# Products of a unit as one run behind its turns, in a fused attention and two-layer feed-forward kernel on one core

## The chip, the core and the metric

The kernel runs on one core of one Trainium2 chip. The metric is the device time of one execution in microseconds (us). The core has five engines that work side by side, each through its own queue in order: PE (TensorE, matrix products; its weight loads are listed apart as PEld), DVE (VectorE), ACT (ScalarE), POOL (GpSimd) and SP (SyncE, which here only issues transfers; its queue is listed as SPq).

## The reference

Decay attention over 4 batches and 8 heads of 576 tokens with 64 features, then two feed-forward layers on the 2304 x 512 result:

```python
scores = scale * q @ k.T + (cum[i] - cum[j])      # cum: running sum of log f; causal mask
attn   = softmax(scores);  x = attn @ v           # heads side by side: 2304 x 512
h = x @ w_in;   g = h * tanh(softplus(h));   y = g @ w_out          # 512 -> 2048 -> 512
m = max(y @ w1, y @ w2, y @ w3);   out = m @ w2_out                 # 512 -> 768 -> 512
```

All of it is fp32, and the feed-forward inputs are split in a high and a low part so that one product is three (`mm3`, L179).

## The kernel before

**Attention.** `attention()` (L437) goes through 16 jobs, a job being one batch and one pair of heads (`U` and `L`: partitions 0 to 63 and 64 to 127), and each job has two units: g = 0 holds query rows 0 to 255, g = 1 the other 320. A unit is made in two halves. `scores` (L334) multiplies q and k into `sc`, DVE adds the decay and finds the row minimum (L386), ACT takes the exponent (L392) and POOL scales by the row sum (L356), which gives tiles `P`. Two units later (`LEAD`) `av` (L400) turns the `P` tiles with PE transposes into banks `pp` (L413, the "turns"; up to four per bank, 6 turns in a unit g = 0, 19 in a unit g = 1), copies each bank to `TA` or `TB` by DVE and ACT in turn (L417, L419), and multiplies with v into the accumulator `av` (L423, the "products"). A product uses 64 columns of the PE array, the lower 64 for head U and the upper 64 for head L; a unit g = 0 has 4 products, a unit g = 1 has 18 (6 of 256 columns, 2 of 128, 10 of 64). The trace lists an fp32 product as two rows (passes), so the 18 products are 36 rows. The finished accumulator is split by ACT and DVE into `xh` and `xl` (L131, L137), the input of the next layer. `prep` (L298) turns the next job's q and k (`tr`, L308 and L310) in each unit g = 0.

**What stands between.** `h_steps` (L475) makes the first layer's `h` (L181 to L183, full-array products) as soon as a block of 512 tokens is complete; two steps follow every unit. Weights come through `load_w_in` (L198): `fetch` issues a transfer on SP (L146), three ahead of use, and `convert` and `split` unpack them on ACT (L156), POOL (L160, L137) and DVE.

**What sets the order.** The code is written unit by unit, and a scheduler orders each engine's instructions by priority and its own estimate; attention has a high priority. `tc.issue_after(x)` (through `queued`, L176) keeps an instruction behind x on the engine. `att_psum` (L228) gives `pp` and `tr` three banks in common; the accumulator has one. After attention the rest runs stage by stage: `h` to its end, `y` (w_out), `g` (three maxima), `q` and `o`.

Of the kernel before, what the change touches and what calls it, by code (L numbers as in the profile page):

```python
# [34 lines left out]
LEAD = 2  # L35
# [25 lines left out]
LAYOUT = [turned_layout(g) for g in range(2)]  # L61
# [3 lines left out]
def tile_decay_attention__mish_ff__max3_ff(  # L65
# [16 lines left out]
    nc = tc.nc  # L82
# [10 lines left out]
    at = ExitStack()  # L93
# [8 lines left out]
    ident = const.tile([128, 128], F32, name="ident")  # L102
# [38 lines left out]
    def fetch(pool, src, bufs):  # L141

        m, n = src.shape[0] // 128, src.shape[1]
        r = pool.tile([128, m, n, 2], I32, name="wr", tag="wr", bufs=bufs)
        with queued(pace):
            nc.sync.dma_start(  # L146
                r.rearrange("p m n w -> p m (n w)"), src.bitcast(I32).rearrange("(m p) w -> p m w", p=128)
            )
        return r

    def convert(pool, r, bufs=None, abs_eng="dve"):

        t = pool.tile([128, r.shape[1], r.shape[2]], F32, name="wt", tag="wt", bufs=bufs)
        lo, hi, ti = r[:, :, :, 0], r[:, :, :, 1], t.bitcast(I32)
        if abs_eng == "act":
            nc.scalar.activation(t, hi.bitcast(F32), AF.Abs)  # L156
        else:
            nc.vector.tensor_scalar(ti, hi, 0x7FFFFFFF, None, op0=ALU.bitwise_and)
        eng = nc.gpsimd if abs_eng == "act" else nc.vector
        eng.tensor_scalar(  # L160
            t, t, F32_MIN_AS_HIGH_HALF, F32_MAX_AS_HIGH_HALF, op0=ALU.max, op1=ALU.min
        )
        nc.vector.tensor_scalar(
            ti, ti, 3, 0x3FFFFFF8, op0=ALU.logical_shift_left, op1=ALU.bitwise_and
        )
        nc.vector.scalar_tensor_tensor(
            out=ti, in0=hi, scalar=-0x40000000, in1=ti,
            op0=ALU.bitwise_and, op1=ALU.bitwise_or,
        )
        nc.vector.scalar_tensor_tensor(  # L170
            out=ti, in0=lo, scalar=29, in1=ti,
            op0=ALU.logical_shift_right, op1=ALU.bitwise_or,
        )
        return t

    def queued(last):  # L176
        return tc.issue_after(last[-1].ins) if last else ExitStack()
# [20 lines left out]
    def load_w_in():  # L198
        jobs = [(fp, c) for fp in range(NFP) for c in range(0, KD, 2)]
        raws = []  # L200
        for k, (fp, c) in enumerate(jobs):
            for f_, c_ in jobs[len(raws):k + 3]:
                raws.append(fetch(wst, moe_w_in[c_ * 128:(c_ + 2) * 128, f_ * 256:f_ * 256 + 256], 4))
            t = convert(wst, raws[k], abs_eng="act")
            split(wi[fp][:, 0, c:c + 2], wi[fp][:, 1, c:c + 2], t, "act", "pool")
            if c + 2 == KD:
                loaded.add(fp)
            yield
# [20 lines left out]
        return aps.tile([128, 512], F32, name=name, tag="ps", bufs=3)  # L229

    U, L = slice(0, 64), slice(64, 128)


    sums = [aw.tile([128, 5], F32, name=f"sums{i}") for i in range(4)]
    raws = [[ap_.tile([128, 640], F32, name=f"raw{c}{i}") for c in "qk"] for i in range(2)]
    vs = [aw.tile([128, 640], F32, name=f"vs{i}") for i in range(3)]
# [61 lines left out]
    def prep(J):  # L298

        b, hp, raw = J["b"], J["hp"], J["raw"]  # L300
        qq = as_.tile([128, 512], F32, name="qT", bufs=2)
        kk = as_.tile([128, S], F32, name="kT", bufs=2)
        last, v_ = q4[J["i"] % 2], vs[J["i"] % 3]
        rest = att_psum("tr")
        for i, dst in ((1, kk), (0, qq)):
            tr = att_psum("tr")
            for c in range(4):
                nc.tensor.transpose(tr[:, c * 128:c * 128 + 128], raw[i][:, c * 128:c * 128 + 128], ident)  # L308
            nc.scalar.activation(dst[:, 0:512], tr, AF.Copy)  # L309
            nc.tensor.transpose(rest[:, i * 64:i * 64 + 64], raw[i][U, 512:640], ident[U, U])  # L310
        nc.scalar.activation(kk[:, 512:S], rest[:, 64:128], AF.Copy)
        for h, rows in enumerate((U, L)):
            nc.scalar.activation(last[rows, h * 64:h * 64 + 64], rest[rows, 0:64], AF.Copy)
        for h in range(2):
            nc.sync.dma_start(
                v_[:, h * 256:(h + 1) * 256].rearrange("p (t d) -> p t d", t=4),
                v[b, 2 * hp + h, 0:512, :].rearrange("(t p) d -> p t d", t=4),
            )
        nc.sync.dma_start(
            v_[L, 512:640].rearrange("p (h d) -> p h d", h=2),  # L320
            v[b, 2 * hp:2 * hp + 2, 512:S, :].rearrange("h p d -> p h d"),
        )
        J.update(q=qq, q4=last, k=kk, vs=v_)
        mask_decay(J)
# [75 lines left out]
    def av(J, g, P):  # L400


        q0 = 0 if g == 0 else 256
        gw = 256 if g == 0 else 320
        T = (TA, TB)[g]
        acc = aps.tile([128, 512], F32, name="av", bufs=1)
        for c, blocks, products in LAYOUT[g]:
            pp = att_psum("pp")
            for n, (kt, h, qt) in enumerate(blocks):

                k0 = kt * 128 if kt < 4 else S - 128
                Pt = P[4] if qt == 4 else P[h, qt]
                nc.tensor.transpose(pp[:, n * 128:n * 128 + 128], Pt[:, k0:k0 + 128], ident)  # L413
            w = len(blocks) * 128
            count["bank"] += 1
            if count["bank"] % 2:
                nc.vector.tensor_copy(T[:, c:c + w], pp[:, :w])  # L417
            else:
                nc.scalar.activation(T[:, c:c + w], pp[:, :w], AF.Copy)  # L419
            for kt, off, w, *at in products:  # L420
                for h in range(2):
                    n = 4 * h + kt if kt < 4 else 8 + h
                    nc.tensor.matmul(  # L423
                        acc[(U, L)[h], off:off + w], J["vs"][:, n * 64:n * 64 + 64], T[:, at[h]:at[h] + w],
                        start=kt == 0 and off == 0, stop=kt == (1 if g == 0 else 4), skip_group_check=True,
                    )
        t0 = J["b"] * S + q0
        at_ = 0
        while at_ < gw:
            blk, off = divmod(t0 + at_, BLK2)  # L430
            n = min(gw - at_, BLK2 - off)
            xh, xl = x_tiles(blk)
            cs = slice(off, off + n)
            pace[:] = [split(xh[:, J["hp"], cs], xl[:, J["hp"], cs], acc[:, at_:at_ + n], "act", "dve")]
            at_ += n

    def attention():  # L437


        jobs = [(b, hp) for b in range(B) for hp in range(H // 2)]  # L440
        J = {0: load(0, *jobs[0])}
        yield 0
        prep(J[0])
        J[1] = load(1, *jobs[1])
        tok = 0
        units = [(ji, g) for ji in range(len(jobs)) for g in range(2)]
        pend = []
        for n in range(len(units) + LEAD):
            if n == 6 + LEAD:
                eps.clear()  # L450
                early.close()
                eps_h.append(sa.enter_context(tc.tile_pool(name="hps", bufs=2, space=PSUM, reuse_waits="tile")))
            if n < len(units):
                ji, g = units[n]
                pend.append((J[ji], g, scores(J[ji], g)))
            if n >= LEAD:
                unit = pend.pop(0)
                av(*unit)
                if unit[0]["hp"] == H // 2 - 1:
                    tok = unit[0]["b"] * S + (256, S)[unit[1]]  # L460
            if n < len(units):
                if g == (ji == 0) and ji + 1 < len(jobs):
                    prep(J[ji + 1])
                if g == 1 and ji + 2 < len(jobs):
                    J[ji + 2] = load(ji + 2, *jobs[ji + 2])
            yield tok
# [46 lines left out]
    credit, na = 0.0, 0  # L513
    while True:

        with tc.high_priority(AHEAD):
            done = next(attn, None)
        if done is None:
            break

        na += 1
        for _ in range(2 if 2 <= na <= 9 else 0):
            next(wgen, None)
        if len(loaded) == NFP and not x4:
            top.close()
            x4.append(top.enter_context(tc.tile_pool(name="x4", bufs=1)))
            x4[0].tile([128, 216], F32, name="gap")
        credit += RATE
        while credit >= 1.0:
            credit -= 1.0  # L530
            if next(steps, None) is None:
                credit = 0.0
# [113 lines left out]
    for step, (ib, fp, a) in enumerate(todo):  # L646
        n = blocks1[ib][1]
# [128 lines left out]
    for ft in range(NF2):  # L776
        g = [gps[ft % 2].tile([128, BLK2], F32, name=f"g{m}") for m in range(3)]
        for m in range(3):
            for c in range(KD):
                w = wa[m][ft // 3, c // 2]  # L780
# [26 lines left out]
    for t0 in (BLK2, BLK2 + 2 * HALF):  # L807
        hh = [hp2.tile([128, 2 * HALF], F32R, name=f"hh{c}") for c in range(NF2)]
        hl = [hp2.tile([128, 2 * HALF], F32R, name=f"hl{c}") for c in range(NF2)]
        for p in range(3):  # L810
# [54 lines left out]
            for i, eng in ((0, "pool"), (2, "dve"), (1, "dve"), (3, "dve")) if p == 2 else ((i, "pool") for i in range(4)):  # L865
                f, h = p + 3 * (i // 2), i % 2
# [37 lines left out]
```

## Time and profile before

| | |
|---|---|
| median of 3 runs | 925.68 us (924.67 to 927.26) |
| profiled execution, its own time | 926.2 us |
| span in its trace | 924.4 us (1.8 us lie around it) |
| instructions | 13929 |
| PE busy | 903.4 us, 98% of the span |
| DVE, ACT, POOL busy | 496.3, 400.1, 234.0 us |

A span is cut in windows below, and a timeline row gives the start, the duration and the number of merged rows. Matmuls overlap their neighbours in the trace, so the time that a row takes from the engine is read from start to next start, not from its duration.

### The profile page before, as it was taken

How to read it: one execution, taken by the hardware profiler on the slowest of the kernel's cores; microseconds unless marked ns; L12 is line 12 of the kernel's file. 1: busy time of each engine (PE TensorE's matmuls, PEld its weight loads, DVE VectorE, ACT ScalarE, POOL GpSimd, SP SyncE). 2: the span in 40 equal slices, each digit the busy share in tenths (PEclk: the TensorE clock that was granted, in tenths of full speed). 3: DMA queues.
4: the chain of work that ended last, by engine and by line, in shares of the span. 5: the costliest groups of instructions: out<-in, count | busy, mean ns of one | idle time of the engine just before them, and what ended most of it. 6: DMA issues, size and time to landing. Idle time of an engine off the chain costs nothing.

```text
span 924.4 us, 13929 instructions
## 1 busy us (share of the span) xinstructions
PE 903.4 (98%) x4800; PEld 711.8 (77%) x4800; DVE 496.3 (54%) x1186; ACT 400.1 (43%) x913; POOL 234.0 (25%) x317
## 2 busy tenths in 40 slices
PE   5898999999999999999999999999999999999998
PEld 3566666666666677889888888889888998889986
DVE  3688665334434442991267757584874455515440
ACT  4786656444444432442556545453443213312211
POOL 3689985222213220000002000000121323013310
PEclk9999999999999999999999999999999999999999
DMA  8896654333332113872365666663599543334401
GB/s 180 230 214 175 198 173 115 102 114 107 105 95 92 61 48 132 306 247 91 126 213 192 212 212 213 209 235 105 164 339 328 157 131 101 117 102 127 126 29 62
DMA packets 125030, 145.25 MB, mean 157 GB/s; under 512 B 64736, under 2 KB 78048, under 8 KB 124960
## 3 DMA queue, kind: packets, MB, share of 16 engines
q1 hardware_dynamic: 105856, 102.41, 37.8%
q10 hardware_dynamic: 16416, 27.79, 8.2%
q0 software_dynamic: 2688, 14.16, 4.2%
q8 instruction: 38, 0.62, 0.3%
q14 instruction: 32, 0.26, 0.1%
HBM read 102.83 MB, written 41.49 MB: 156 GB/s over the span
## 4 chain that ended last, share of the span: by engine, by line
PE 94%; DVE 2%; DMA 2%; issue 1%; ACT 1%; SPq 1%; DVEq 0%
PE h L181 8%; PE h L182 7%; PE h L183 7%; PE y L183 7%; PE y L181 7%; PE y L182 7%; PE av L423 7%; PE sc L332 6%; PE pp L413 6%; PE q L182 5%; PE q L183 5%; PE q L181 5%; PE o L181 3%; PE o L182 3%; PE o L183 2%; PE tr L308 2%
## 5 line engine op out<-in xcount | busy, mean ns | idle before, releaser
L182 PE MATMUL h<-xl,wi 128*128 128x512 f32 (+1 forms) x320 | 120.6, 377 | 1.8 <-DVE xl L137 1.8
L181 PE MATMUL h<-xh,wi 128*128 128x512 f32 (+1 forms) x320 | 122.0, 382 | 0.0
L183 PE MATMUL h<-xh,wi 128*128 128x512 f32 (+1 forms) x320 | 120.2, 376 | 0.0
L182 PE MATMUL y<-gl,wo 128*128 128x512 f32 (+1 forms) x320 | 117.7, 368 | 0.0
L183 PE MATMUL y<-gh,wo 128*128 128x512 f32 (+1 forms) x320 | 117.6, 368 | 0.0
L181 PE MATMUL y<-gh,wo 128*128 128x512 f32 (+1 forms) x320 | 106.3, 368 | 0.0
L638 DVE TENSOR_TENSOR gl<-g,gh 128x512 fp32r<-128x512 f32 x72 | 49.9, 695 | 91.7 <-ACT gh L637 91.3
L356 POOL TENSOR_SCALAR P<-P,rr 128x128 f32<-128x128 f32 (+3 forms) x128 | 74.8, 598 | 95.3 <-DVE rr L354 54.1
L392 ACT ACTIVATE P<-P,mn 128x128 f32<-128x128 f32 (+3 forms) x128 | 70.6, 554 | 62.6 <-DVE mn L386 62.6
L631 ACT ACTIVATE g<-g 128x512 f32<-128x512 f32 x72 | 45.4, 633 | 76.4 <-DMA g<-h_d 70.5
L182 PEld LDWEIGHTS h<-xl,wi 128*128 128x128 f32 x320 | 60.2, 188 | 12.9 <-issue 2.2
L181 PEld LDWEIGHTS h<-xh,wi 128*128 128x128 f32 x320 | 60.0, 188 | 12.7 <-issue 2.8
L183 PEld LDWEIGHTS h<-xh,wi 128*128 128x128 f32 x320 | 60.4, 189 | 10.5 <-issue 1.3
L182 PEld LDWEIGHTS y<-gl,wo 128*128 128x128 f32 x320 | 60.3, 188 | 10.2
L183 PEld LDWEIGHTS y<-gh,wo 128*128 128x128 f32 x320 | 60.3, 189 | 10.1
L181 PEld LDWEIGHTS y<-gh,wo 128*128 128x128 f32 x320 | 60.3, 189 | 10.1
L413 PE MATMUL pp<-ident,P 128*128 128x128 f32 x320 | 57.7, 290 | 3.6 <-ACT qT L309 3.6
L423 PE MATMUL av<-TB,vs 128*64 128x64 f32 (+2 forms) x576 | 60.4, 294 | 0.3 <-DVE xl L137 0.3
L413 PEld LDWEIGHTS pp<-ident,P 128*128 128x128 f32 x320 | 38.1, 143 | 24.6 <-issue 8.9
L830 DVE TENSOR_TENSOR u<-q,p 128x448 f32<-128x448 f32 x36 | 22.4, 622 | 63.2 <-PE q L183 63.2
L501 ACT ACTIVATE he<-h 128x512 f32<-128x512 f32 x56 | 33.1, 593 | 49.5 <-PE h L183 49.5
L423 PEld LDWEIGHTS av<-TB,vs 128*64 128x64 f32 x576 | 34.9, 136 | 25.3 <-issue 9.7
(141 smaller groups left out, 1880.6 us busy)
## 6 DMA issues: line engine op xcount, KB each, us to landing
g<-h_d SPq DMA_DIRECT2D x72, 256.0 KB, 2.9
s<-s_d SPq DMA_DIRECT2D x72, 256.0 KB, 2.9
h_d<-he ACTq DMA_DIRECT2D x56, 256.0 KB, 2.7
wr<-in_moe_w_out_dram SPq DMA_DIRECT2D x22, 512.0 KB, 4.4
wr<-in_moe_w_dram SPq DMA_DIRECT2D x24, 384.0 KB, 3.7
s_d<-sk POOLq DMA_DIRECT2D x12, 768.0 KB, 5.7
cb<-cum_d SPq DMA_DIRECT2D x32, 256.0 KB, 4.2
wr<-in_moe_w_in_dram SPq DMA_DIRECT2D x16, 512.0 KB, 4.4
```

What stands on the lines that cost most here:

```text
L181: nc.tensor.matmul(ps, wh, xh, start=start, stop=False, skip_group_check=True)
L182: nc.tensor.matmul(ps, wh, xl, start=False, stop=False, skip_group_check=True)
L183: return nc.tensor.matmul(ps, wl, xh, start=False, stop=stop, skip_group_check=True)
L332: nc.tensor.matmul(dst, lhs, J["k"][rows, c0:c0 + w], start=True, stop=True, skip_group_check=True)
L356: nc.gpsimd.tensor_scalar(made[ci], made[ci], rr[:, ci:ci + 1], 1.0, op0=ALU.mult, op1=ALU.mult)
L392: nc.scalar.activation(Pt, Pt, AF.Exp, scale=-1.0, bias=mn[:, col - 1:col], accum_out=sm[:, ci:ci + 1],)
L413: nc.tensor.transpose(pp[:, n * 128:n * 128 + 128], Pt[:, k0:k0 + 128], ident)
L423: nc.tensor.matmul(acc[(U, L)[h], off:off + w], J["vs"][:, n * 64:n * 64 + 64], T[:, at[h]:at[h] + w], start=kt == 0 and off == 0, stop=kt ...
L501: nc.scalar.activation(he, h, AF.Copy)
L631: nc.scalar.activation(g, g, AF.Mish)
L638: on_dve[:] = [nc.vector.tensor_tensor(out=gl, in0=g, in1=gh, op=ALU.subtract)]
L830: add = lambda eng, o, x, y: eng.tensor_tensor(out=o, in0=x, in1=y, op=ALU.add)
```

## The change

The change has two parts. In batches 1 to 3 a unit's products are no longer emitted bank by bank between its turns, but all together after its last turn, and, where the unit also holds a `prep`, after that `prep`'s last transposes (`last_tr`). The next unit's turns and `prep` transposes are issued behind the last of these products (`last_av`). In batch 0 (`together` is false) the products stay bank by bank. `prep`'s two 64-row transposes are now emitted ahead of the ACT copy and in the same queue hold. The second part lets `load_w_in` issue its first three transfers and then pause, in the first step of the main loop, where before nothing was done; the conversions keep their steps.

```diff
@@ load_w_in
             for f_, c_ in jobs[len(raws):k + 3]:
                 raws.append(fetch(wst, moe_w_in[c_ * 128:(c_ + 2) * 128, f_ * 256:f_ * 256 + 256], 4))
+            if k == 0:
+                yield
             t = convert(wst, raws[k], abs_eng="act")
@@ prep
-            for c in range(4):
-                nc.tensor.transpose(tr[:, c * 128:c * 128 + 128], raw[i][:, c * 128:c * 128 + 128], ident)
+            with queued(last_av):
+                for c in range(4):
+                    nc.tensor.transpose(tr[:, c * 128:c * 128 + 128], raw[i][:, c * 128:c * 128 + 128], ident)
+                last_tr[:] = [nc.tensor.transpose(rest[:, i * 64:i * 64 + 64], raw[i][U, 512:640], ident[U, U])]
             nc.scalar.activation(dst[:, 0:512], tr, AF.Copy)
-            nc.tensor.transpose(rest[:, i * 64:i * 64 + 64], raw[i][U, 512:640], ident[U, U])
@@ av
+        def multiply(products):
+            for kt, off, w, *at in products:
+                for h in range(2):
+                    n = 4 * h + kt if kt < 4 else 8 + h
+                    last = nc.tensor.matmul(
+                        acc[(U, L)[h], off:off + w], J["vs"][:, n * 64:n * 64 + 64], T[:, at[h]:at[h] + w],
+                        start=kt == 0 and off == 0, stop=kt == (1 if g == 0 else 4), skip_group_check=True,
+                    )
+            return last
+
+        together = J["b"] > 0
...
-                nc.tensor.transpose(pp[:, n * 128:n * 128 + 128], Pt[:, k0:k0 + 128], ident)
+                with queued(last_av):
+                    turn = nc.tensor.transpose(pp[:, n * 128:n * 128 + 128], Pt[:, k0:k0 + 128], ident)
...
+            if not together:
+                multiply(products)
+        yield
+        if together:
+            with tc.issue_after((last_tr or [turn])[-1].ins):
+                last_av[:] = [multiply([p for *_, products in LAYOUT[g] for p in products])]
@@ attention
-                av(*unit)
+                rest = av(*unit)
+                next(rest)
+                if unit[0]["b"] == 0:
+                    next(rest, None)
+            last_tr.clear()
+            if n < len(units) and g == (ji == 0) and ji + 1 < len(jobs):
+                prep(J[ji + 1])
+            if n >= LEAD:
+                next(rest, None)
@@ main loop
-        for _ in range(2 if 2 <= na <= 9 else 0):
+        for _ in range(2 if 2 <= na <= 9 else na == 1):
             next(wgen, None)
```

How the instructions stand on the engines shows the rest. On PE, one unit g = 1 of batch 2: before, the last 12 of its 18 products stood among the next unit's turns `pp` and `prep`'s `tr`:

```order
L332 MATMUL sc<-kT,q_0_188 128x288 x2
L423 MATMUL av<-TB,vs_179 64x128 x2
L423 MATMUL av<-TB,vs_179 64x64 x2
L413 MATMUL pp<-ident,P_0_2499 128x128
L423 MATMUL av<-TB,vs_179 64x64
L413 MATMUL pp<-ident,P_1_2502 128x128
L423 MATMUL av<-TB,vs_179 64x64 x2
L308 MATMUL tr<-ident,rawk_176 128x128
L423 MATMUL av<-TB,vs_179 64x64
```

Five more such alternations follow there. Of the same unit's last 12 products the changed order on PE makes one stretch, behind the same scores:

```order
L181 MATMUL h<-xh_589,wi_150 128x512
L336 MATMUL sc<-kT,q_0_188 128x288 x2
L415 MATMUL av<-TB,vs_179 64x128 x2
L415 MATMUL av<-TB,vs_179 64x64 x10
L429 MATMUL pp<-ident,P_0_2484 128x128
L429 MATMUL pp<-ident,P_0_2499 128x128
```

The next unit's turns have moved behind the products, and the `tr` rows too. Over the whole program PE has 122 unbroken stretches of products before and 65 now; batch 0 holds 21 of the 122 and 20 of the 65.

On SP, where the first words of w_in (L146) stand among the loads of q, k and the decay, before:

```order
L269 DMA cb<-cum_d 128x2x256 x2
L259 DMA rawq_175<-in_q_dram 64x2x64
L272 DMA cb_602<-cum_d 64x576 x2
L146 DMA wr<-in_moe_w_in_dram 128x2x512 x4
L255 DMA rawk_178<-in_k_dram 128x4x64 x2
```

The changed order of SP at the same place (row 40 of the queue in both):

```order
L272 DMA cb<-cum_d 128x2x256 x2
L262 DMA rawq_175<-in_q_dram 64x2x64
L275 DMA cb_602<-cum_d 64x576 x2
L146 DMA wr<-in_moe_w_in_dram 128x2x512 x4
L258 DMA rawk_178<-in_k_dram 128x4x64 x2
```

Apart from line numbers nothing moved there: the four transfers stand behind the same loads.

## Rows read from the trace of the kernel before

**Rows 1.** The page's part 1, busy time of each engine.

```profile
PE 903.4 (98%) x4800; PEld 711.8 (77%) x4800; DVE 496.3 (54%) x1186; ACT 400.1 (43%) x913; POOL 234.0 (25%) x317
```

**Rows 2.** PE's waits, longest first: total us, times, longest.

```profile
PE tr L308 <- DMA rawk<-in_k_dram: 4.2, 1, 4.2
PE pp L413 <- ACT qT L309: 3.6, 1, 3.6
```

**Rows 3.** Windows: each engine's busy us and rows, granted clock, DMA share, GB/s.

```profile
75.00:100.00 25.00, 22.05 (x148) 15.55 (x147) 20.23 (x55) 17.64 (x49) 23.75 (x27) 0.93 0.76 208
100.00:364.00 264.00, 264.00 (x1576) 179.33 (x1575) 118.69 (x394) 120.42 (x341) 98.00 (x143) 1.00 0.34 104
```

**Rows 4.** Timeline of PE, one unit's products cut in eight: start, duration, rows.

```profile
215.74 0.27 PE L413 MATMUL pp<-ident,P_None 128*128 128x128 f32 x1
215.94 1.52 PE L423 MATMUL av<-TB,vs 128*64 128x256 f32 x12
217.38 1.13 PE L332 MATMUL sc<-kT,qT 64*128 64x512 f32 x4
...
224.08 0.55 PE L423 MATMUL av<-TB,vs 128*64 128x128 f32 x8
224.57 0.33 PE L413 MATMUL pp<-ident,P 128*128 128x128 f32 x1
224.83 0.33 PE L423 MATMUL av<-TB,vs 128*64 128x64 f32 x2
225.09 0.33 PE L413 MATMUL pp<-ident,P 128*128 128x128 f32 x1
225.34 0.34 PE L423 MATMUL av<-TB,vs 128*64 128x64 f32 x4
225.61 0.33 PE L308 MATMUL tr<-ident,rawk 128*128 128x128 f32 x1
...
227.69 0.27 PE L310 MATMUL tr<-ident,rawk 64*128 64x64 f32 x1
```

**Rows 5.** Timeline of PE, another unit's products in one piece, then twelve turns.

```profile
87.48 2.31 PE L423 MATMUL av<-TB,vs 128*64 128x256 f32 x36
89.73 1.13 PE L332 MATMUL sc<-kT,qT 64*128 64x512 f32 x4
90.79 1.53 PE L413 MATMUL pp<-ident,P 128*128 128x128 f32 x12
92.07 0.71 PE L181 MATMUL h<-xh,wi 128*128 128x512 f32 x2
```

**Rows 6.** Timeline of PE, twelve 64-column passes in one stretch.

```profile
363.02 0.57 PE L423 MATMUL av<-TB,vs 128*64 128x64 f32 x12
363.52 0.50 PE L182 MATMUL h<-xl,wi 128*128 128x512 f32 x1
```

**Rows 7.** Groups by line and shape: count, busy us, mean ns, idle before.

```profile
L417 DVE COPY TB<-pp 128x512 f32<-128x512 f32 x32 | 21.8, 684 | 7.3 <-PE pp L413 7.1
L137 DVE TENSOR_TENSOR xl<-av,xh 128x256 fp32r<-128x256 f32 x24 | 9.9, 413 | 6.9 <-ACT xh L131 6.8
L131 ACT ACTIVATE xh<-av 128x256 fp32r<-128x256 f32 x24 | 9.1, 378 | 6.5 <-PE av L423 5.4 <-DVE xl L137 0.6 <-PE pp L413 0.4
```

**Rows 8.** Timeline of SP's queue and of ACT around the first w_in transfers.

```profile
37.05 1.19 SPq L272 DMA_DIRECT2D cb<-cum_d  x2
38.29 2.43 SPq L146 DMA_DIRECT2D wr<-in_moe_w_in_dram  x4
...
42.63 0.67 ACT L156 ACTIVATE wt<-wr 128x512 f32<-128x512 f32 x1 [3.83 <-DMA wr<-in_moe_w_in_dram]
```

**Rows 9.** Window of the w_in conversions, columns as in rows 3.

```profile
100.00:150.00 50.00, 50.00 (x287) 32.03 (x285) 34.95 (x91) 29.66 (x78) 44.00 (x40) 1.00 0.50 146
```

**Rows 10.** Windows of the twelve turns and of the lowest clock, columns as before.

```profile
90.79:92.07 1.28, 1.28 (x14) 1.28 (x13) 1.21 (x5) 0.52 (x3) 1.28 (x3) 1.00 0.91 195
46.42:49.83 3.41, 3.41 (x19) 2.41 (x15) 3.41 (x11) 2.85 (x9) 2.25 (x3) 0.50 1.04 205
```

More of the change, by code (lines that the diff above doesn't have):

```diff
@@ L231, in tile_decay_attention__mish_ff__max3_ff @@
     U, L = slice(0, 64), slice(64, 128)
+    last_av, last_tr = [], []
     sums = [aw.tile([128, 5], F32, name=f"sums{i}") for i in range(4)]
@@ L419, in av @@
                 nc.scalar.activation(T[:, c:c + w], pp[:, :w], AF.Copy)
[L420 to L426, printed above, removed]
+            if not together:
[4 more added lines that the diff above has]
+                last_av[:] = [multiply([p for *_, products in LAYOUT[g] for p in products])]
         t0 = J["b"] * S + q0
@@ L461, in attention @@
             if n < len(units):
-                if g == (ji == 0) and ji + 1 < len(jobs):
-                    prep(J[ji + 1])
                 if g == 1 and ji + 2 < len(jobs):
```

## The prediction

> **What bounds the kernel now.** I read the page's busy shares first: PE is busy 98% of the span and no other engine more than 54% [rows 1]. That is an average, so the windows come next: from 100 to 364 us, which is attention of batches 1 to 3 with the first layer's products between, PE is busy all 264.00 us [rows 3]. Its list of waits says the same from the other side: the long ones (4.2 us for the first k, 3.6 us for ACT's qT) all lie in the first 100 us [rows 2]. So from 100 us on no engine makes PE wait, and time can only come from PE needing less of it for the same work. A busy PE is not a PE at its peak, though, so the third view is PE's timeline, read from start to next start. It holds the same kind of work in two arrangements, and the reader is to compare them.
>
> In the first, a unit g = 1 has its 36 passes in eight stretches, cut by scores and by single turns [rows 4]. In the second, a unit of batch 0 happened to get its 36 passes in one piece [rows 5]. The one piece takes 89.73 - 87.48 = 2.25 us. The cut unit takes 217.38 - 215.94 = 1.44 us for the first stretch, and 227.69 - 224.08 = 3.61 us for the other seven with six turns among them. Twelve turns in a row take 92.07 - 90.79 = 1.28 us [rows 5], 0.107 each, so the six are worth 0.64 and the products 2.97. Together that is 4.41 us against 2.25, for the same 18 products: seven more stretches cost 2.16 us, **0.31 us a stretch**.
>
> Where it goes can be seen in the same rows. At the start of a stretch: a turn that is alone before a product takes 224.83 - 224.57 = 0.26 us from the engine instead of 0.107, so 0.15 more; a turn that ends a longer row takes 215.94 - 215.74 = 0.20, so 0.09 more [rows 4]. At its end: four 64-column passes take 225.61 - 225.34 = 0.27 us [rows 4] and twelve take 363.52 - 363.02 = 0.50 [rows 6], which is 0.029 for each further pass and thus 0.155 that a stretch pays once, whatever its length. Ends and starts sum to 0.25 us (after a row of turns) to 0.31 (after a single turn). A stretch of one product is worse: its two passes take 225.09 - 224.83 = 0.26 us [rows 4], of which 0.06 are the passes, so 0.20 at its end and 0.15 at its start are 0.35. This gives the price of a removed stretch a low bound of 0.25, a high one of 0.35, and 0.31 from the whole unit, which has the mix of long and short stretches that the change removes. I take 0.31.
>
> **The change part by part.** *Products as one run.* The work itself stays: the same turns, products, copies and splits. What is removed is alternation. By the two orders PE has 122 stretches of products before and 65 now; 21 and 20 of them are in batch 0, so 101 become 45 in the part where PE never waits, 56 fewer. (It is not one stretch for each of the 24 units, 24 in all, since scores and first-layer products still fall between.) 56 x 0.31 = **17.4 us**; by the bounds 56 x 0.25 = 14.0 and 56 x 0.35 = 19.6.
>
> *What the run now waits for.* The products stand behind the unit's last turn, and the next unit's turns behind the products. Queued behind a late run are therefore the next turns, then the bank copies on DVE and ACT, then the next products. A bank's copy takes 0.68 us on DVE, the split of the accumulator 0.38 on ACT and 0.41 on DVE [rows 7]. Three places could pay. First, the reader of the last bank: in each unit g = 1 of the changed order the first twelve products, two or more scores or first-layer rows among them, stand between the last turn and the first product that reads that bank. Six 256-column products alone take 1.44 us [rows 4], twice the copy; the copy is hidden, and without that cover would cost 0.68. Second, units g = 0: ten transposes of `prep` (the eight full ones alone take 8 x 0.107 = 0.86 us) or 18 and more first-layer rows stand between turns and products; hidden as well. Third, the accumulator: its split of 0.79 us must end before the next run starts, and all turns of that unit stand between (6 x 0.107 = 0.64 us at least, with scores and first-layer rows among them). So I cost the new waits at nothing, with 0 to 4 us as bounds, the upper being five or six uncovered copies. After the last product 398 first-layer rows follow instead of 431, so the work that covered nothing at the end has moved forward as cover, and less of it is left.
>
> *POOL.* Between 100 and 150 us POOL is busy 44.0 of 50 us with w_in and with P [rows 9]. A faster PE could run into it there. By the orders, PE has 12 fewer stretches in front of the first turn of unit 14 (about 156 us), worth 3.7 us, but 136 first-layer rows in front of it instead of 110. It reaches those turns no sooner, and POOL's own order keeps its sixteen w_in splits within two P tiles of where they were. I cost it at nothing; if the cover fails, 3.7 us are lost.
>
> *First words of w_in one step earlier.* The code asks for it, and the place where it would pay is plain: the transfers are issued at 38.29 us, behind the loads of q, k and decay, ACT's queue stands 3.83 us at the first conversion [rows 8], and PE waits 3.6 us for the qT copy queued behind it [rows 2]; afterwards the granted clock is 0.50 for 3.41 us [rows 10], which at half speed costs 1.7 more. But the order of SP is the same up to and beyond these four transfers, and so is that of ACT up to the conversions and of PE up to about 72 us. Nothing of the start can move: 0 us, and 5.3 if it did.
>
> *The sum.* 17.4 from the stretches, 0 for waits and 0 for the fetch. The profiled execution took 926.2 us (its span 924.4 and 1.8 around it): 926.2 - 17.4 = 908.8. The median of the runs is 925.68, 0.5 lower, so the forecast for the median is **908 us**, by the bounds 906 (all at 0.35) to 916 (0.25 and 4 us of waits).
>
> **The rivals.** (1) *The fetch works after all*, for instance because the transfers land earlier without another order: 908.3 - 5.3 = 903. Against it stand the unchanged queues. (2) *New waits take part of the gain.* The scheduler's own times are not the chip's; if each of the twelve units g = 1 waits out one copy, 12 x 0.68 = 8.2 us go, and the time is 916 to 917. For it speaks that turns and products can no longer fill each other's waits; against it that PE waits nowhere in 264 us now and that first-layer rows still stand in every gap. POOL's 3.7 us belong here too (912). (3) *Slower:* the turns, copies, run and split of each unit become one chain, with copy and split open to PE: 0.68 + 0.38 + 0.41 = 1.47 us in each of 24 units, 35.3 us, thus 944. It turns a gain to a loss from 17.4 / 24 = 0.73 us a unit. It needs the gaps without other PE work, and the order shows none such before the last unit. [...] (5) *No gain:* the price of a stretch is only how the trace models the ends of matmuls. Against it: starts, not ends, were used, and the sums of starts make up the span. Then 925.7.
>
> **How the numbers follow.** Forecast 0.74; fetch 0.06; part of the gain lost 0.12; slower by the chain 0.03; clock 0.02; no gain 0.03. The first three are faster (0.92), the last the same (0.03), the chain and the clock slower (0.05); 0.3%, about 3 us, is what a measurement of this kernel can tell from no change. The likeliest case alone spans 906 to 916; the range takes rival 2 in at the top (917) and part of rival 1 at the bottom (904), and leaves out what is left.
>
> **What would show each step.** The products' rows in the timeline come in long stretches, and units g = 1 take about 2.3 us plus some 0.25 for each further cut. PE stays fully busy from 100 us to the end of attention, which then comes sooner, and `y`, `g`, `q` and `o` keep their durations, only earlier. PE's wait of 3.6 us for qT stays, with the lower clock after it. I am wrong in the price if PE is as full as before and the time falls by much other than 17 us; wrong on the waits if PE's list shows new ones for TA, TB, `xl` or P beyond 4 us; wrong on the fetch if the 3.6 us are gone.

## The result and the profile after

The changed kernel takes **909.62 us** (908.35 to 912.03, 4 runs) against 925.71 for the one before (4 runs on the same chip): a ratio of 0.983, with a 95% interval of 0.9816 to 0.9844, that is 16.1 us less. The profiled execution took 909.78 us, its span is 907.7. One kernel below (products together from batch 2 on) was profiled in an execution of 1448.94 us at a granted clock of 0.562, which its median leaves out.

First the page of after: its part 1, as in [rows 1], and the first line of its chain.

```profile
PE 882.8 (97%) x4800; PEld 704.8 (78%) x4800; DVE 497.1 (55%) x1186; ACT 400.7 (44%) x913; POOL 232.7 (26%) x317
PE 89%; POOL 3%; DMA 2%; DVE 2%; issue 1%; ACT 1%; SPq 1%; POOLq 0%
```

PE is busy 20.6 us less with the same 4800 instructions [rows 1]. The span shrank by 16.7, so some 4 us of what PE no longer needs are now spent idle. Where it idles is in its list of waits, of which these are the lines that bear on the change (total, times, longest):

```profile
PE pp L429 <- ACT qT L314: 3.6, 1, 3.6
PE sc L336 <- DVE mn L390: 3.3, 2, 2.0
PE h L181 <- ACT he L522: 1.3, 1, 1.3
PE pp L429 <- DVE TB L433: 0.6, 1, 0.6
```

The first is the wait of [rows 2], unchanged. The second is new, a wait of the scores for DVE (2.00 us at 106.83 us, the other 1.25 at 85.13, in batch 0). The third is new too, and the last is the only wait for a bank's copy. Three windows of after, the first two as in [rows 3] (attention now ends some 9 us sooner), the third as in [rows 10]:

```profile
75.00:100.00 25.00, 21.50 (x154) 15.01 (x152) 20.82 (x56) 17.81 (x51) 22.82 (x25) 1.00 0.76 210
100.00:346.00 246.00, 242.10 (x1544) 172.39 (x1541) 117.68 (x391) 119.55 (x340) 97.52 (x145) 1.00 0.38 112
45.10:52.00 6.90, 6.62 (x27) 4.37 (x27) 6.63 (x22) 6.25 (x21) 4.74 (x6) 0.51 1.04 240
```

From 100 us on PE was never idle before [rows 3]; now it is idle 246.00 - 242.10 = 3.9 us. The granted clock is 1.00 through all of it. Behind the wait for qT the lower clock lasts 6.90 us here and 3.41 before [rows 10]; in return the window from 75 to 100 us has 1.00 instead of 0.93.

PE's timeline of after, a unit g = 1 with its products in two stretches, as in [rows 4]:

```profile
149.07 1.52 PE L415 MATMUL av<-TB,vs 128*64 128x256 f32 x12
...
153.26 0.93 PE L336 MATMUL sc<-kT,qT 64*128 64x128 f32 x8
154.12 1.02 PE L415 MATMUL av<-TB,vs 128*64 128x128 f32 x24
155.07 0.87 PE L429 MATMUL pp<-ident,P 128*128 128x128 f32 x6
```

The 24 passes take 155.07 - 154.12 = 0.95 us, and the twelve ahead of them 1.45 to their next start: 2.40 us for what took 4.41 before, the six turns among it taken out at 0.107 each [rows 4, 5].

**The account.** I added up PE's rows by kind in both traces, each from its start to the next start with idle time taken out, from the end of the last product of batch 0 to the first row of `y`. This part holds the same 528 rows of products and 942 of the first layer in both.

| us | before | after | change |
|---|---|---|---|
| products (101 and 45 stretches) | 51.3 | 40.7 | -10.6 |
| turns and `tr` | 51.0 | 42.9 | -8.1 |
| scores | 42.1 | 40.1 | -2.0 |
| first layer | 206.7 | 207.2 | +0.5 |
| PE idle | 0.0 | 4.1 | +4.1 |
| sum | 351.1 | 335.0 | -16.1 |

So 56 fewer stretches gave 20.2 us of PE's time, 0.36 each, and new waits took 4.1 back, which leaves 16.1 / 56 = 0.29 net. Ahead of this part the two traces differ by 0.4 us. From the first row of `y` to the end both traces take the same: 483.53 us and 483.37.

**Where the waits come from.** The largest first. PE's timeline of after around 104 us:

```profile
99.65 0.65 PE L415 MATMUL av<-TB,vs 128*64 128x256 f32 x4
100.24 0.93 PE L336 MATMUL sc<-kT,qT 64*128 64x128 f32 x8
...
103.93 0.90 PE L415 MATMUL av<-TB,vs 128*64 128x128 f32 x20
106.83 0.88 PE L336 MATMUL sc<-kT,qT 64*128 64x384 f32 x2 [2.00 <-DVE mn L390]
```

After 104.83 PE has nothing ahead of the next scores, and these wait, by the releaser that the row names, for DVE's row minimum (L390), behind which a bank of `sc` comes free. POOL's and then DVE's timeline at that moment:

```profile
98.72 2.30 POOL L295 TENSOR_SCALAR_AFFINE_SELECT cb<-cb 128x512 f32<-128x512 f32 x3 [0.93 <-DMA cb<-cum_d]
101.01 1.91 POOL L160 TENSOR_SCALAR wt<-wt 128x512 f32<-128x512 f32 x1
```

```profile
102.95 0.43 DVE L163 TENSOR_SCALAR wt<-wt 128x512 int32<-128x512 int32 x1 [2.50 <-POOL wt L160]
103.30 0.55 DVE L433 COPY TB<-pp 128x384 f32<-128x384 f32 x1
103.76 0.71 DVE L166 SCALAR_TENSOR_TENSOR wt<-wr,wt 128x512 int32<-128x512 int32 x1
104.51 1.06 DVE L170 SCALAR_TENSOR_TENSOR wt<-wr,wt 128x512 int32<-128x512 int32 x1
105.50 0.28 DVE L390 CUSTOM_DVE_ANT_0 P<-sc,cb 128x128 f32<-128x128 f32 x1
```

DVE stands 2.50 us at a word of w_in that POOL clips behind a mask whose decay came late. The row minima are queued behind this word's three operations, and PE stands.

The other two waits from 100 us on hang on such words as well. PE's wait of 1.32 us is for ACT, whose copy `he` (L522) empties a bank of `h`. ACT stands 1.63 us at a word that DVE has not finished, with the copy queued behind it:

```profile
145.97 0.50 PE L181 MATMUL h<-xh,wi 128*128 128x512 f32 x1 [1.32 <-ACT he L522]
```

```profile
144.80 0.63 ACT L131 ACTIVATE wi<-wt 128x512 fp32r<-128x512 f32 x1 [1.63 <-DVE wt L170]
145.34 0.58 ACT L522 ACTIVATE he<-h 128x512 f32<-128x512 f32 x1
```

And the copy of a bank for which PE waits 0.58 us at 125.04 stands in DVE's queue behind a word at which DVE had waited 3.20 us for POOL's clip:

```profile
121.84 0.43 DVE L163 TENSOR_SCALAR wt<-wt 128x512 int32<-128x512 int32 x1 [3.20 <-POOL wt L160]
...
124.30 0.69 DVE L433 COPY TB<-pp 128x512 f32<-128x512 f32 x1
```

### The profile page after: what moved, and what is told of

The parts are those of the page before. It is cut to its first block, busy times and chain, and to the rows that moved or that the text cites. A ratio compares the mean times of both kernels' runs of the same rounds, so it can differ in the third digit from the quotient of the medians.

```text
span 907.7 us, 13930 instructions
## 1 busy us (share of the span) xinstructions
PE 882.8 (97%) x4800; PEld 704.8 (78%) x4800; DVE 497.1 (55%) x1186; ACT 400.7 (44%) x913; POOL 232.7 (26%) x317
## 4 chain that ended last, share of the span: by engine, by line
PE 89%; POOL 3%; DMA 2%; DVE 2%; issue 1%; ACT 1%; SPq 1%; POOLq 0%
PE y L181 7%; PE y L183 7%; PE y L182 7%; PE h L181 7%; PE h L182 7%; PE h L183 7%; PE q L182 6%; PE q L183 6%; PE q L181 6%; PE sc L336 5%; PE av L415 5%; PE pp L429 5%; PE o L181 3%; PE o L182 3%; PE o L183 3%; PE g L181 2%
## 5 line engine op out<-in xcount | busy, mean ns | idle before, releaser
L181 PEld LDWEIGHTS h<-xh,wi 128*128 128x128 f32 x320 | 60.1, 188 | 14.6 <-issue 2.2
L182 PEld LDWEIGHTS y<-gl,wo 128*128 128x128 f32 x320 | 60.3, 188 | 10.2
L522 ACT ACTIVATE he<-h 128x512 f32<-128x512 f32 x56 | 33.3, 595 | 57.0 <-PE h L183 52.4
L336 PE MATMUL sc<-kT,qT 64*128 64x128 f32 (+3 forms) x256 | 51.9, 500 | 3.6 <-DVE mn L390 3.3
L429 PE MATMUL pp<-ident,P 128*128 128x128 f32 x320 | 51.1, 285 | 4.0 <-ACT qT L314 3.6
L658 ACT ACTIVATE gh<-g 128x512 fp32r<-128x512 f32 x72 | 45.0, 627 | 22.0 <-PE y L183 20.9
```

Source lines behind the costliest of these rows:

```text
L181: nc.tensor.matmul(ps, wh, xh, start=start, stop=False, skip_group_check=True)
L182: nc.tensor.matmul(ps, wh, xl, start=False, stop=False, skip_group_check=True)
L336: nc.tensor.matmul(dst, lhs, J["k"][rows, c0:c0 + w], start=True, stop=True, skip_group_check=True)
L429: turn = nc.tensor.transpose(pp[:, n * 128:n * 128 + 128], Pt[:, k0:k0 + 128], ident)
L522: nc.scalar.activation(he, h, AF.Copy)
L658: on_act[:] = [nc.scalar.activation(gh, g, AF.Copy)]
```

## The experiments

The theory: a stretch of products costs PE about 0.31 us, and what is missing from the gain is waits behind the words of w_in. The rivals: the price is an artefact of the records or depends on where the cut falls; the waits come from elsewhere. The chip's time of before lay between 924.9 and 925.9 us throughout.

### The price of a cut: the same spare turns, ahead of the run and inside it

Four spare turns go into each of the 12 runs of the units g = 1, in one kernel ahead of the run, in the other between its last 64-column pairs.

```diff
+        def spare():
+            return nc.tensor.matmul(acc[:, 384:512], ident, ident, start=False, stop=False, is_transpose=True, ...)
         def multiply(products, spares=0):
...
+                if CUT and 5 <= k < 5 + spares:      # inside
+                    last = spare()
+                elif not CUT and k == 0:             # ahead
+                    for _ in range(spares): spare()
```

> The changed kernel with four spare turns ahead of the first product of each of the 12 runs of a unit g = 1; 61 stretches. Both theories: 48 x 0.107 = 5.1 us for the turns themselves, less 4 stretches, thus 909.6 + 5.1 - 1.2 = 913.5.

> The changed kernel with four spare turns (a transpose of the identity into columns of the accumulator that nobody reads) in each of the 12 runs of a unit g = 1, each between two 64-column products; 110 stretches. To be read against the kernel with the same 48 spare turns ahead of the runs (61 stretches). Theory: 49 more stretches at 0.31 us are 15 us more than that kernel, by the bounds 12 to 17: about 930. Rival (a cut costs nothing of itself, only the turn's own 0.107 us counts): no difference between the two, both about 915.

Ahead: 913.83 us (913.64 to 914.25), ratio 0.9877 [0.9862, 0.9892]. Inside: 927.71 (925.83 to 928.77, 10 runs), ratio 1.0024 [1.0015, 1.0034]. The same turns and products with 110 stretches instead of 61 cost 13.9 us, **0.28 us a cut**: the price is real time. PE's timeline of the kernel with the turns inside:

```profile
152.77 0.55 PE L429 MATMUL av<-TB,vs 128*64 128x128 f32 x8
153.26 0.33 PE L413 MATMUL av<-ident 128*128 128x128 f32 x1
153.51 0.34 PE L429 MATMUL av<-TB,vs 128*64 128x64 f32 x4
153.78 0.33 PE L413 MATMUL av<-ident 128*128 128x128 f32 x1
154.04 0.34 PE L429 MATMUL av<-TB,vs 128*64 128x64 f32 x4
```

Each spare turn takes 0.25 to 0.26 us from the engine, each pair (four passes) 0.27, as [rows 4] had it. By the account above the products take 7.5 us more than with the turns ahead (49 x 0.155 = 7.6). The 0.28 is a net price, as the 0.29 above: in the account the kernel with the turns inside idles 3.3 us less (1.5 against 4.9) and loses some 1.7 us to 3.41 us at a clock of 0.50 (from 110.49 us). Without both, 12.9 us more there become 14.5 us of PE's time, 0.30 a cut.

### Where the cut falls: between the heads of a pair

The account showed that single products have a price of their own. This kernel, set here against the one with the turns inside, has the four spare turns of each run between and behind the halves U and L of two 256-column pairs.

```diff
-                if CUT and 5 <= k < 5 + spares:
+                    if spares and 3 <= 2 * k + h < 3 + spares:   # ahead of L1, U2, L2, U3
```

> As in the run with spare turns inside, each of the 12 runs of the units g = 1 is cut by four spare turns, and PE has about as many stretches (109 against 110), but here the four cuts fall between U and L of two 256-column pairs and behind each of their halves, instead of between 64-column pairs. Theory: the products of U and L of one pair run side by side on the two halves of the columns, so a stretch that holds one product alone lasts as long as one that holds the pair (in the trace of the changed kernel the four passes of a 256-column pair take 0.59 us, in that of before two passes alone 0.58). A split pair then costs its product once more, 0.58 - 0.155 = 0.43 us; 24 split pairs are 10.2 us, and the time is 938 (936 to 940). Rival: a cut has one price wherever it falls, and the time is that of the other run, 927.7 (926 to 929.5).

Measured 937.16 us (936.25 to 937.94), ratio 1.0134 [1.0117, 1.0151], 9.5 us above the other run, where 10.2 were expected and the rival gave none. In the account its products take 9.4 us more. Its timeline of PE:

```profile
150.19 0.33 PE L412 MATMUL av<-ident 128*128 128x128 f32 x1
150.45 0.65 PE L425 MATMUL av<-TB,vs 128*64 128x256 f32 x2
151.03 0.33 PE L412 MATMUL av<-ident 128*128 128x128 f32 x1
151.29 0.65 PE L425 MATMUL av<-TB,vs 128*64 128x256 f32 x2
151.86 0.33 PE L412 MATMUL av<-ident 128*128 128x128 f32 x1
```

One product alone (two passes) takes 151.03 - 150.45 = 0.58 us; a whole pair took 100.24 - 99.65 = 0.59 in after. So the products of the two heads run side by side, and a cut between them costs the product a second time. With 0.155 us a stretch and 0.43, 0.21 or 0.11 us for each pair or lone product of 256, 128 or 64 columns ((1.44 - 0.58) / 2 by [rows 4] and the rows above; 126.06 - 125.69 - 0.155 for a lone product in the trace of before; (0.50 - 0.27) / 2 by [rows 4, 6]), with each stretch taken as long as the half of the array that has more to do in it, all products together come to 51.3 us in before, 40.1 in after and 57.3 here, where the traces have 51.3, 40.7 and 57.3. Before, 31 stretches began with the second half of a pair, after it 5.

### No hold on the next unit's turns

```diff
-                last_av[:] = [multiply([p for *_, products in LAYOUT[g] for p in products])]
+                multiply([p for *_, products in LAYOUT[g] for p in products])
```

> The changed kernel, but the next unit's turns and prep transposes are not held behind the run; products are still emitted together. PE's order then has 149 stretches of products, against 65 in the changed kernel and 122 before. Theory (the price is the stretch, 0.31 us): 84 more than in the changed kernel, 26 us, less the changed kernel's new waits of about 4 us, thus 909.6 + 26 - 4 = 932, slower than before. Rival (emitting a unit's products together is what helps, wherever they end up on PE): 906 to 912.

Measured 943.11 us (941.76 to 943.44), ratio 1.019 [1.0175, 1.0205], worse than forecast. Without the hold the scheduler cuts the run more often than before, 149 stretches, and 61 of those in the account begin with a second half. The products take 64.1 us instead of before's 51.3, and PE is busy all 260.00 us from 100 to 360 us. So the gain needs the hold; the order in which the code is written does not bring it alone.

### Together from batch 2 on

```diff
-        together = J["b"] > 0
+        together = J["b"] > 1
...
```

> The changed kernel with the products together in batches 2 and 3 alone; 90 stretches, 25 more than in the changed kernel. Theory: 25 stretches at 0.35 us come back, 8.8 us, and the waits of 2.0, 0.6 and 1.3 us in batch 1, where the w_in words are converted beside the runs, go: 909.6 + 8.8 - 3.9 = 914.5. Rival (the waits have nothing to do with runs beside words): 918.4.

Measured 916.73 us, ratio 0.9901 [0.9885, 0.9918], from three executions, none of them profiled. It lies between both forecasts. PE has 90 stretches, and per stretch both steps are worth the same: 925.76 - 916.73 = 9.0 for 32, 0.28 each, and 916.73 - 909.62 = 7.1 for 25, 0.28 each. Batch 1, where the waits are, pays no worse than the others; what it loses in waits can't be told from these times.

### The run also behind the first-layer rows of its step

```diff
-            with tc.issue_after((last_tr or [turn])[-1].ins):
+            with tc.issue_after((last_tr or [turn])[-1].ins), queued(last_h):
...
-                    mm3(
+                    last_h[:] = [mm3(
...
+                if unit[0]["b"] > 0:
+                    yield tok
...
-        credit += RATE
+        credit += RATE if na <= 10 else RATE / 2
```

So that such rows stand ahead of the run, attention pauses for them once more in each unit of batches 1 to 3, and from the eleventh pause on one step follows a pause instead of two.

> The changed kernel with each run of batches 1 to 3 also held behind the first-layer products of its step, so that these fill the time of the bank copies and the run stays whole: 48 stretches on PE, 27 of them behind batch 0 instead of 45. Theory (the price is the stretch, 0.31 to 0.35 us): 18 fewer are 5.6 to 6.3 us less, thus 903 to 904, if the waits stay as they are. Rival (the longer hold delays turns, copies and scores and PE waits): 908 to 915, with new rows in PE's list of waits.

Measured 911.33 us (910.16 to 913.61), ratio 0.985 [0.9829, 0.9871]: a miss. There are 27 stretches behind batch 0 instead of 45, no pair is split, and yet the part in the account takes 335 us, as in after. Products take 2.8 us less (18 x 0.155) and scores 3.4, but first-layer rows 2.9, turns 1.9 and idle time 1.2 more (5.3 in all, 1.7 of them right behind batch 0). In part that is the clock. PE's timeline and a window of this kernel:

```profile
142.49 0.66 PE L312 MATMUL tr<-ident,rawq 128*128 128x128 f32 x4 [1.48 <-DVE TA L433]
```

```profile
144.10:147.50 3.40, 3.40 (x14) 1.85 (x13) 3.20 (x6) 2.10 (x6) 2.65 (x3) 0.50 0.24 81
```

After a wait for a bank the clock is 0.50 for 3.40 us, some 1.7 us lost. The rest I can't place: removing cuts made by scores and first-layer rows did not bring what removing cuts made by turns did.

### The waits: clip on DVE, no words on DVE, conversions spread out

Three kernels go at the words of w_in. One moves POOL's clip to DVE:

```diff
-        eng = nc.gpsimd if abs_eng == "act" else nc.vector
-        eng.tensor_scalar(
+        nc.vector.tensor_scalar(
```

> The changed kernel with the clip of the w_in words (L160) on DVE instead of POOL; 65 stretches as before. Theory: PE's three new waits of batch 1 (2.0, 0.6 and 1.3 us) come from DVE standing behind a w_in word that POOL has not clipped yet; with the clip on DVE they go, about 4 us, thus 905 to 906. Rival (the waits come from the run itself, turns and products no longer filling each other's gaps): the waits stay, 909 to 911, or DVE's 7 us more work adds to them.

Measured 915.41 us (914.64 to 917.72), ratio 0.9897 [0.988, 0.9914]: 5.8 us worse instead of better. Its list of PE's waits and its DVE at 94 us:

```profile
PE sc L335 <- DVE mn L389: 6.3, 4, 2.0
```

```profile
94.11 0.40 DVE L159 TENSOR_SCALAR wt<-wt 128x512 f32<-128x512 f32 x1
94.55 0.70 DVE L162 TENSOR_SCALAR wt<-wt 128x512 int32<-128x512 int32 x1
95.28 0.95 DVE L165 SCALAR_TENSOR_TENSOR wt<-wr,wt 128x512 int32<-128x512 int32 x1
96.16 0.68 DVE L389 CUSTOM_DVE_ANT_1 P<-sc,cb 128x512 f32<-128x512 f32 x1
```

The wait of DVE for POOL's clip is gone, and PE's wait for the minima has grown from 3.3 to 6.3 us over the whole span, with the words now back to back ahead of the minima. But the loss lies early. The last product of batch 0 ends at 95.62 us, in after at 89.36; from there to `y` both take 335.0 us. Ahead of it PE waits 1.02 us at 72.32 and 1.89 at 90.62 for minima, and the clock is 0.50 for 3.41 us from 74.51 and again from 91.57. From 100 us on the kernel does what the theory said:

```profile
100.00:346.00 246.00, 244.63 (x1554) 176.26 (x1555) 116.71 (x394) 120.00 (x340) 78.23 (x136) 0.99 0.37 110
```

PE is idle 1.4 us there, in after 3.9. So POOL's clip has a part in those waits, and on DVE it costs more before them than it gives.

The second leaves out DVE's three operations on each of these words, in the changed kernel, so that the first layer's weights are no longer w_in:

```diff
+        if abs_eng == "act":
+            return t
         nc.vector.tensor_scalar(
```

> The changed kernel without the three DVE operations on each w_in word (L163, L166, L170: the shift and the two merges), so the weights of the first layer are not w_in; ACT's and POOL's part of the conversion stays. 57 stretches. Theory: PE's waits between 80 and 150 us (1.3, 2.0, 0.6, 1.3 us) are DVE standing in w_in words while attention's row minima queue behind; they go, 5 us, and 8 fewer stretches are worth up to 2 more: 902 to 905. Rival (the waits belong to the run): they stay, 907 to 910.

Measured 903.62 us (903.13 to 904.5), ratio 0.9757 [0.974, 0.9774]. Its window answers to that of after:

```profile
100.00:346.00 246.00, 246.00 (x1571) 177.55 (x1565) 100.54 (x354) 118.23 (x329) 84.21 (x137) 1.00 0.36 106
```

PE is busy all 246.00 us: the waits of this part of attention hang on DVE's words. Are they new with the change? The same edit in the kernel before:

> The kernel before without the three DVE operations on each w_in word (its first layer's weights are not w_in), to be read against the changed kernel without them, 903.6; 107 stretches against 57. Theory: without the words neither kernel waits between 90 and 350 us, so the difference of the two is the stretches alone, 50 x 0.35 = 17.5 us: about 921. Rival (the words cost the kernel before as much as the changed one): 919 or less, the difference staying at 16 or under.

Measured 919.6 us (919.28 to 920.14), ratio 0.9935 [0.992, 0.995]. The words cost the kernel before as much, 925.8 - 919.6 = 6.2 us, as the changed one, 909.6 - 903.6 = 6.0, and between these two kernels the change is worth 16.0 us, as it is with words (50 stretches, 0.32 each). So "the words take back 4 us of this gain" is not shown: without them the order of PE comes out with 10 fewer stretches in before (91 in the account) and 4 fewer in after (41), so before seems to lose to its words mostly by more cuts (it never idles in the account), and after mostly by waits (4.1 us of idle time in the account, 1.2 without the words).

The third spreads the conversions over 16 units instead of 8:

```diff
-        for _ in range(2 if 2 <= na <= 9 else na == 1):
+        for _ in range(1 if 1 <= na <= 17 else 0):
```

> The changed kernel with one w_in conversion emitted per unit instead of two, over 16 units instead of 8, which stretches the words' work on DVE and POOL; 64 stretches. Theory: DVE stands less in words in each unit, so the 5 us of waits between 80 and 150 us shrink: 905 to 909. Rival (first-layer products then wait for their weights, or the words only meet the later units): 910 to 914.

Measured 908.82 us (907.73 to 909.86), ratio 0.9812 [0.9794, 0.983]: not to be told from the changed kernel. Waits of the scores for DVE remain (1.44 us at 126 us), and the clock falls to 0.50 for 3.4 us after that one.

### The fetch, made to happen

Of the change's second part alone I built a kernel and read its order: on all five engines it is row for row that of before, waits included, and the first part alone gives the order of the changed kernel. So the second part does nothing in the built program; neither of the two was timed. This kernel makes it happen, with the first three transfers ten places earlier in SP's queue:

```diff
+        if na == 1:
+            with tc.high_priority(AHEAD - 100):
+                next(wgen, None)
-        for _ in range(2 if 2 <= na <= 9 else na == 1):
+        for _ in range(2 if 2 <= na <= 9 else 0):
```

> The changed kernel with its first three w_in transfers given nearly attention's priority, so that SP issues them ten rows sooner, behind the loads of the third job instead of the fourth's; 66 stretches. Theory (the change's own fetch moved nothing; a fetch that does move takes PE's wait of 3.6 us for qT and the half clock behind it, 1.7 us, away): 909.6 - 5.3 = 904. Rival (the words then reach POOL and DVE sooner and PE waits for these instead): 907 to 911.

Measured 910.31 us (908.88 to 910.7), ratio 0.9825 [0.9808, 0.9843]: no gain. Its timelines of PE and ACT:

```profile
47.40 1.23 PE L336 MATMUL sc<-kT,qT 64*128 64x128 f32 x6 [3.57 <-ACT qT L314]
```

```profile
45.40 0.66 ACT L156 ACTIVATE wt<-wr 128x512 f32<-128x512 f32 x1
45.96 0.71 ACT L396 ACTIVATE P<-P,mn 128x512 f32<-128x512 f32 x1
46.58 0.19 ACT L396 ACTIVATION_READ_ACCUMULATOR P<-P,mn 128x1 f32 x1
46.67 0.20 ACT L131 ACTIVATE xh<-av 128x64 fp32r<-128x64 f32 x1
46.77 0.58 ACT L314 ACTIVATE qT<-tr 128x512 f32<-128x512 f32 x1
```

ACT no longer stands at the conversion, but the qT copy has other work ahead of it, and PE waits for it as long as before, only 2 us later; the clock is 0.50 from 46.4 to 56.6 us, 10.2 us where after has 6.9.

### Together in batch 0 too

```diff
-        together = J["b"] > 0
+        together = True
...
```

> The changed kernel with the products together in batch 0 too: 59 stretches, 13 of them in batch 0 instead of 20. Theory: PE is not the bound in the first 100 us, where it waits for transfers, ACT and DVE, so 7 fewer stretches (2 us) show only in part: 908 to 910. Rival (a hold where PE has no first-layer products to fill with costs waits): 911 to 915.

Measured 914.44 us (912.33 to 917.41), ratio 0.9877 [0.9846, 0.9908]: 4.8 us worse than the changed kernel with 6 fewer stretches. PE's idle time in the first 80 us grows from 14.6 to 17.8 us, with a wait of 3.0 for a bank's copy (`TA`) that the hold exposes. The wait comes at 41.39 us, and the first first-layer row, which could cover it, only at 59.73. The last product of batch 0 ends 1.1 us later than in the changed kernel, and the part in the account takes 3.5 us more, 1.7 of them for 16 turns that have moved into it (at 0.107 each).

## Why the prediction came true, point by point

**The price, 0.31 us by 56 stretches.** The count was right (101 to 45), the price too low: 20.2 / 56 = 0.36, above its upper bound of 0.35, 20.2 us instead of 17.4. Of these 2.8 us products bring 1.9 more than 56 x 0.155 = 8.7, and scores 2.0 that were not counted; turns bring 0.6 less than 8.7, and first-layer rows take 0.5. The end of a stretch costs 0.155 us, as predicted: with the turns inside the products take 7.5 us more for 49 stretches, 0.153 each. What the sum lacked is the split pair: of two passes at 0.26 and four at 0.27 [rows 4] the prediction made 0.029 for each pass and a longer end (0.20) for the shorter stretch, where they say that the second head's product takes no time of its own beside the first. It had only 64-column pairs before it, where that is 0.11 us; of 256 columns it is 0.43. With 26 fewer stretches that begin on a second half this is worth 2.6 us by the prices above (3.4 us in before, 0.8 in after). Turns gave 8.1 us, 0.14 a stretch, within the 0.09 to 0.15 of the prediction. In the traces half a pair of 256 columns takes 0.58 us and a whole one 0.59.

**The new waits, costed at nothing (0 to 4).** This step failed in size: 4.1 us in the account, at its upper bound. It also looked in the wrong places. Of its three, only the bank's copy shows, with 0.58 us; the accumulator's split holds up no run (0.24 us at 90.66 us are first-layer rows that wait for `xh`). The two largest, 2.00 us of the scores for DVE and 1.32 of the first layer for ACT, were not among them: PE reaches these rows while DVE, or ACT behind it, still stands in words of w_in. Rival 2, twelve copies of 0.68, did not happen.

**The two errors offset**: 2.8 us too little gain and 4.1 too little loss leave a net of 16.1 instead of 17.4, and 909.6 instead of 908. The mechanism was right; that the number came this close is in part luck.

**POOL at nothing.** PE's own waits for POOL are 0.3 us in all. POOL's lateness came to PE by way of DVE.

**The fetch at nothing.** Right, and for the reason given: the order of the queues is the same, and the wait for qT is still 3.6 us. The 5.3 us that it was worth "if it did move" are wrong: moved, it brought nothing.

**The rivals.** The chain of copy, run and split does not show: no wait of the products or of the next run for the accumulator is in the list. That the clock falls through the turns, to which the prediction gave a chance of 0.02, is not shown: in after it is granted at 1.00 from 75 to 346 us, with rows of up to twelve turns. "No gain, only modelled ends" is refuted by 16.1 us less, and by 13.9 us for 49 cuts.

**What stays open**: why cuts by scores and first-layer rows cost so little in sum when they go, and how much of the 4.1 us of idle time could be had without paying for it in another order.

## What to carry to other kernels

Where small products share the array with transposes, count PE's changes between them and read the price from start to next start (here 0.28 to 0.36 us a stretch); the busy share of 98% did not show it. Keep the products that run side by side together first of all, since a cut between them costs one of them whole (here 0.58 us for half a pair of 256 columns, where the pair takes 0.59). And when PE gets faster, look at what stands in the queue of the engine that empties its banks, not only at the copies that the change itself moves.

## What the runs showed of the hardware

Two products that use 64 columns of the array each, one on either half, took the time of one: with 256 columns of data 0.58 us for one alone (turns between the heads of a pair, at 150.45 us) and 0.59 for both (after, at 99.65). How long PE waited did not by itself decide whether its clock fell in attention. It was granted 0.50 for 3.40 us after a wait of 1.48 us (run behind first-layer rows, from 144.10 us) and 0.51 over 6.90 us at the end of one of 3.6 us (after, from 45.10), while after the 2.00 us that end at 106.83 in after it kept 1.00.
